# Four tiles for raw weights instead of two, each load issued four half units ahead

## The chip, the cores and the metric

The kernel runs on one core of one Trainium2 chip. The time is that of one execution on the device, in microseconds (us); the timed runs are three, and their median counts. The trace is of one further execution, the profiled one, which has a time of its own. Engines are named as the profile does: PE (TensorE, with its weight loads as PEld), DVE (VectorE), ACT (ScalarE), POOL (GpSimd), SP (SyncE, which here only issues DMA transfers).

## What is computed

Attention whose scores are mixed over the heads before and after the softmax, for 4 batches, 12 heads, 448 positions and a head size of 64, and behind it a two-layer network with a PReLU on the 1792 rows of 768 numbers that attention gives. `w_in` and `w_out` come as float64, all else as float32.

```python
scores = scale * np.matmul(q, k.transpose(0, 1, 3, 2))
scores = np.einsum('bhij,hg->bgij', scores, w_pre)
scores = scores - np.max(scores, axis=-1, keepdims=True)
attn = np.exp(scores)
attn = attn / (np.sum(attn, axis=-1, keepdims=True) + 1e-09)
attn = np.einsum('bhij,hg->bgij', attn, w_post)
attn_out = np.matmul(attn, v).astype(np.float32)
x = np.ascontiguousarray(attn_out.transpose(0, 2, 1, 3)).reshape(B * S, H * D)
h = x @ w_in
g = np.maximum(h, 0.0) + alpha * np.minimum(h, 0.0)
out = (g @ w_out).astype(np.float32)
```

## The kernel before

**Three kinds of work in one program.** The order of the instructions on every engine is fixed by the order of the code; each engine works in that order and waits where a tile isn't ready. The code is one loop over steps n (`step`). A step does one block of attention: the head mix on PE into PSUM (`mix`, L205), the negated maximum on DVE (`nm`, L207), the exponentials on ACT (`exp`, L214), for the block before it the scales on DVE (`norm`, L221 to L225), for the block two before it the second mix on PE (`post`, L238) and its copy on ACT (L244). Some steps have a QK product (L177) with its copy (L181, on ACT or DVE), and some a product with V (`pv`, L261), whose two halves of positions are copied by ACT (L267) and added by DVE (`xe`, L268). The scores go from one layout to the other by SBUF-to-SBUF transfers that SP issues (`relay`, `sr<-st`, four or more a step).

**The network** (`moe`) runs in tasks of one batch each, a few matmuls at a time between the parts of a step, from step `ready[0]` on; a table of paces (`PACE`) says how much per step. Its first layer is L394, its second L427; the weights come from a DRAM scratch `wsc` by `load_w` (`wr`, issued by POOL) and are split into two parts by ACT (L340) and POOL (`ws`, L341). DVE does the PReLU (`t`, L348 and L349, and L355) and sums the output (`acc`, L363).

**The conversion** (`convert`, `round_f64`) turns the float64 weights into float32 in `wsc`. It is cut into 64 half units: 16 blocks f, two weights x (0 is `w_in`, 1 is `w_out`), two halves c of 384 columns. A half unit has a raw tile `cr` (128 partitions of 384 float64, 384 KB in all), an exponent tile `ce` and a result tile `ct`. Its instructions: L60 (DVE, reads `cr`), L61 and L62 (POOL, on `ce`) with L64 (DVE, reads `cr`, writes `ct`), L65 (DVE, reads `cr`), L66 (DVE, the last to read `cr`), L67 (DVE, finishes `ct`). The generator yields five pieces a unit; a step before `ready[0]` takes 7 of them (`CONV_LEAD`), one after it 8 (`CONV_T0`). The pieces of neighbouring units are interleaved: L60 and L64 of unit i, then L66 and L67 of unit i - 1, then L65 of unit i.

With the L67 of unit i two transfers are tied. Its store to `wsc` (192 KB, L299) is put in a list and issued by SP at the end of the step (`flush`), behind the relays of that step. Its successor's load (`fetch_c`, L289) is issued by POOL at this place of the code, so behind L61 and L62 of unit i + 1; it must wait until the L66 of unit i has read the tile that it overwrites. The pool `cvp` has two tiles each for `cr`, `ce` and `ct`. So L60 of unit i + 2 waits for the load issued behind unit i, and L64 of unit i + 2 for the store of unit i.

POOL also issues, in the same program order, the loads of `q`, `k`, `v` and `wr`. SP issues the stores of `xe`, the loads of `xr` and the output.

Of the kernel before, what the change touches and what calls it, by code (L numbers as in the profile page):

```python
# [12 lines left out]
I64 = mybir.dt.int64  # L13
# [32 lines left out]
CU = DM // 2  # L46
# [3 lines left out]
def round_f64(nc, raw, e, t):  # L50

    w = raw.bitcast(I32).rearrange("p (n t) -> p n t", t=2)
    lo, hi = w[:, :, 0], w[:, :, 1]
    tf = t.bitcast(F32)
    v, g = nc.vector, nc.gpsimd

    yield lambda: v.tensor_scalar(out=e, in0=hi, scalar1=0x7FF00000, scalar2=None, op0=ALU.bitwise_and)  # L60
    g_clamp = lambda: g.tensor_scalar(out=e, in0=e, scalar1=float(1150 << 20), scalar2=float(916 << 20), op0=ALU.min, op1=ALU.max)  # L61
    g_scale = lambda: g.tensor_scalar(out=e, in0=e, scalar1=float(-(916 << 20)), scalar2=8.0, op0=ALU.add, op1=ALU.mult)  # L62
    yield lambda: (g_clamp(), g_scale(),
                   v.tensor_scalar(out=t, in0=hi, scalar1=0xFFFFF, scalar2=0x100000, op0=ALU.bitwise_and, op1=ALU.bitwise_or))  # L64
    yield lambda: v.scalar_tensor_tensor(out=tf, in0=lo.bitcast(U32), scalar=2.0 ** -32, in1=t, op0=ALU.mult, op1=ALU.add)  # L65
    yield lambda: v.scalar_tensor_tensor(out=e, in0=hi, scalar=-0x80000000, in1=e, op0=ALU.bitwise_and, op1=ALU.bitwise_or)  # L66
    yield lambda: v.tensor_tensor(tf, tf, e.bitcast(F32), ALU.mult)  # L67
# [3 lines left out]
def talking_heads_prelu(ctx: ExitStack, tc: tile.TileContext, q, k, v, w_pre, w_post, mask, w_in, w_out, alpha, out):  # L71
# [47 lines left out]
    cvp = pool("cvp", 2)  # L119
# [161 lines left out]
    def convert():  # L281
        todo = [(f, x, c) for f in range(NFC) for x in range(2) for c in range(0, DM, CU)]
        raw_c = {}

        def fetch_c(i):
            if i < len(todo):
                f, x, c = todo[i]
                raw_c[i] = cvp.tile([128, CU], I64, tag="cr", name=f"cr{f}_{x}_{c}")
                nc.gpsimd.dma_start(out=raw_c[i], in_=(w_in, w_out)[x][f, :, c:c + CU])  # L289

        def unit(i):
            f, x, c = todo[i]
            raw = raw_c.pop(i)
            e = cvp.tile([128, CU], I32, tag="ce", name=f"ce{f}_{x}_{c}")
            t = cvp.tile([128, CU], I32, tag="ct", name=f"ct{f}_{x}_{c}")
            for j, op in enumerate(round_f64(nc, raw, e, t)):
                op()
                if j == 4:
                    later.append(lambda: (stored.add((f, x, c)), nc.sync.dma_start(out=wsc[f, :, x * DM + c:x * DM + c + CU], in_=t.bitcast(F32))))  # L299
                    fetch_c(i + 2)  # L300
                yield

        fetch_c(0)
        fetch_c(1)
        yield
        n = len(todo)
        seq = []
        for i in range(n + 1):
            seq += [(i, 0), (i, 1)] if i < n else []
            seq += [(i - 1, 3), (i - 1, 4)] if i else []  # L310
            seq += [(i, 2)] if i < n else []
        units = {}
        for i, j in seq:
            if j == 0:
                units[i] = unit(i)
            next(units[i], None)
            yield
# [156 lines left out]
    with tc.manual_schedule():  # L474
# [41 lines left out]
        load_q(1)  # L516
        nc.gpsimd.dma_start(out=alpha_sb, in_=alpha)
        conv = convert()
        relayed = 0

# [136 lines left out]
```

## Time and profile before

| | us |
|---|---|
| timed runs: median (lowest to highest) | 1153.49 (1153.07 to 1157.48) |
| the profiled execution: time | 1158.48 |
| its span, from the first to the last instruction | 1156.7 |
| PE busy with matmuls (share of the span) | 911.7 (79%) |
| DVE busy | 605.3 (52%) |
| POOL busy | 486.9 (42%) |
| ACT busy | 422.0 (36%) |
| mean granted clock of PE, as a share of full speed | 0.876 |

The profile's page follows the chain of work that ended last back from the last instruction: each step of it is what released the step after it. By lines its largest shares are PE at L427 (17%) and L394 (16%), then the load `cr<-in_w_in_dram` (8%), the load `cr<-in_w_out_dram` (7%), PE at L238 (5%). In the rows further below, a time in square brackets behind an instruction is the idle time of its engine just before it, with what ended it; numbers of tiles are left out there (`cr` is any tile of that name). In a row of the timeline the first number is the start in us and the second the duration. An engine that is not named as waiting may still be idle because nothing was left in its order.

### The profile page before, as it was taken

To read this page: it belongs to the slowest core of one execution; us is meant where nothing else is said; L and a number is where in the kernel's file an instruction comes from. 1 tells how busy PE (TensorE), PEld (TensorE's weight loads), DVE (VectorE), ACT (ScalarE), POOL (GpSimd) and SP (SyncE) were. 2 spreads that over 40 slices of the span, in tenths; PEclk is the share of its full clock that TensorE was granted. 3 is DMA by queue.
4 is the path that set the end of the run, shared out by engine and by line. 5 is a ranking of instruction groups with operands and counts; after the bars stand their busy time and mean duration, and the time that the engine had idled before them with its cause. 6 is when DMAs were issued, how large, how long until landed. Compare 5 with 4: busy or idle time off the path is not lost.

```text
span 1156.7 us, 28915 instructions
## 1 busy us (share of the span) xinstructions
PE 911.7 (79%) x12204; PEld 711.3 (61%) x12204; DVE 605.3 (52%) x1090; ACT 422.0 (36%) x769; POOL 486.9 (42%) x563
## 2 busy tenths in 40 slices
PE   6446565364677766396989999999899999989997
PEld 3224343243454544364866878778678788869996
DVE  4456565553476455457554644463565445445443
ACT  2223333222133223143553555554264544313330
POOL 5332333324154434345342455443253334437662
PEclk8667676875688897698998999999899999989999
DMA  6654456456445445445464446444463333334322
GB/s 168 181 155 144 145 154 179 146 151 195 138 131 154 143 136 150 133 133 160 133 182 162 135 129 167 126 137 147 125 191 124 112 114 108 94 122 122 109 82 76
DMA packets 79730, 161.82 MB, mean 140 GB/s; under 512 B 26276, under 2 KB 64304, under 8 KB 79600
## 3 DMA queue, kind: packets, MB, share of 16 engines
q0 software_dynamic: 21312, 90.58, 29.3%
q1 hardware_dynamic: 57432, 68.18, 17.5%
q8 instruction: 96, 1.57, 0.6%
q10 hardware_dynamic: 856, 1.21, 0.4%
q14 instruction: 34, 0.28, 0.1%
HBM read 97.62 MB, written 23.59 MB: 105 GB/s over the span
## 4 chain that ended last, share of the span: by engine, by line
PE 49%; DMA 22%; DVE 10%; POOL 9%; issue 6%; ACT 1%; SPq 1%; POOLq 0%; ACTq 0%; DVEq 0%
PE p L427 17%; PE p L394 16%; DMA cr<-in_w_in_dram 8%; DMA cr<-in_w_out_dram 7%; PE p L238 5%; PE p L261 4%; POOL ws L341 4%; PE p L205 4%; PE p L177 3%; DMA wsc<-ct 3%; DMA sr<-st 2%; POOL ce L62 2%; DVE nm L207 2%; POOL ce L61 1%; DVE ce L60 1%
## 5 line engine op out<-in xcount | busy, mean ns | idle before, releaser
L341 POOL TENSOR_TENSOR ws<-wr,ws 128x768 fp32r<-128x768 f32 x128 | 235.8, 1843 | 283.6 <-ACT ws L340 281.8
L427 PE MATMUL p<-g,ws 128*128 128x448 f32 x1152 | 259.2, 379 | 21.6 <-POOL ws L341 14.1
L394 PE MATMUL p<-xs,ws 128*128 128x448 f32 x1152 | 262.2, 382 | 12.9 <-DVE xs L449 10.5
L427 PEld LDWEIGHTS p<-g,ws 128*128 128x128 f32 x1152 | 221.3, 195 | 62.0 <-POOL ws L341 18.4
L394 PEld LDWEIGHTS p<-xs,ws 128*128 128x128 f32 x1152 | 220.0, 195 | 57.9 <-issue 21.7
L238 PEld LDWEIGHTS p<-r,e 64*64 64x64 f32 x5040 | 120.2, 157 | 135.6 <-issue 70.7
L238 PE MATMUL p<-r,e 64*64 64x60 f32 x5040 | 125.5, 248 | 91.0 <-DVE r L225 36.3
L214 ACT ACTIVATE e<-p,nm 128x448 f32<-128x448 f32 x180 | 112.6, 633 | 228.1 <-DVE nm L207 172.7
L244 ACT COPY at<-p 128x960 f32<-128x960 f32 x88 | 86.4, 982 | 190.6 <-PE p L238 190.6
L340 ACT CAST ws<-wr 128x768 fp32r<-128x768 f32 x128 | 103.9, 844 | 122.9 <-issue 49.5
L205 PE MATMUL p<-sr,wk 64*64 64x448 f32 (+1 forms) x720 | 106.2, 627 | 53.3 <-ACT e L214 15.5
L207 DVE TENSOR_REDUCE nm<-p 128x2 f32<-128x896 f32 x90 | 97.6, 1084 | 87.0 <-PE p L205 87.0
L177 PE MATMUL p<-k,q 64*64 64x448 f32 x768 | 118.8, 674 | 30.6 <-DVE t L349 21.5
L60 DVE TENSOR_SCALAR ce<-cr 128x384 int32<-128x384 int32 x64 | 28.3, 442 | 208.9 <-DMA cr<-in_w_in_dram 129.9
L363 DVE TENSOR_TENSOR acc<-p,acc 128x896 f32<-128x896 f32 x84 | 91.3, 1087 | 87.9 <-PE p L427 87.7
L61 POOL TENSOR_SCALAR ce<-ce 128x384 int32<-128x384 int32 x64 | 34.8, 543 | 215.8 <-DVE ce L60 215.2
L261 PE MATMUL p<-at,v 64*64 64x120 f32 (+2 forms) x3360 | 98.5, 266 | 29.2 <-ACT e L214 22.9
L261 PEld LDWEIGHTS p<-at,v 64*64 64x64 f32 x3360 | 96.2, 148 | 41.0 <-ACT e L214 26.3
L348 DVE TENSOR_SCALAR t<-p,alpha_sb 128x448 f32<-128x448 f32 x64 | 43.4, 679 | 94.0 <-PE p L394 94.0
L332 POOL DMA_DIRECT2D wr<-wsc x128 | 71.9, 562 | 40.2 <-POOL ws L341 34.7
L205 PEld LDWEIGHTS p<-sr,wk 64*64 64x64 f32 (+1 forms) x720 | 29.8, 150 | 92.1 <-issue 32.5
L181 ACT COPY st<-p 128x896 f32<-128x896 f32 x84 | 74.9, 911 | 11.3 <-PE p L177 6.5
(48 smaller groups left out, 663.7 us busy)
## 6 DMA issues: line engine op xcount, KB each, us to landing
wr<-wsc POOLq DMA_DIRECT2D x128, 384.0 KB, 3.6
sr<-st SPq DMA_DIRECT2D x332, 105.0 KB
cr<-in_w_in_dram POOLq DMA_DIRECT2D x32, 384.0 KB, 4.1
cr<-in_w_out_dram POOLq DMA_DIRECT2D x32, 384.0 KB, 4.1
wsc<-ct SPq DMA_DIRECT2D x64, 192.0 KB
xr<-x SPq DMA_DIRECT2D x24, 224.0 KB
out_dram<-acc SPq DMA_DIRECT2D x12, 448.0 KB
q<-in_q_dram POOLq DMA_DIRECT2D x54, 90.0 KB, 3.7
```

Of the source, the lines that this page charges most:

```text
L177: nc.tensor.matmul(pt[64 * cc:64 * cc + 64, r, :S], q_t[ci][h, (3 * cc + p) * cn + SR0 * cc:(3 * cc + p) * cn + SR0 * cc + 64], k_t[b, p][ ...
L205: nc.tensor.matmul(to[hf:hf + 64, u, :S], wk[r, :], g[r, :], start=True, stop=True)
L207: nc.vector.tensor_reduce(out=nm, in_=to[:, :, :S], axis=AX.X, op=ALU.max, negate=True)
L214: nc.scalar.activation(out=e_t[n][:, u], in_=m_t[n][:, u, :S], func=AF.Exp, bias=nm_t[n][:, u:u + 1], scale=1.0, accum_out=se_t[n][:, u:u ...
L238: nc.tensor.matmul(dst[:, :, HI * u:HI * u + HI], e[h, u, 64 * jb:64 * jb + 64], r[h, u].rearrange("p (h i) -> p h i", h=H), start=True, s ...
L244: nc.scalar.copy(at[:, :, col:col + 2 * GI].rearrange("p q (g i) -> p g q i", g=2), pt[:, :, :NS * GP].rearrange("p g (q i) -> p g q i", i ...
L261: nc.tensor.matmul(to[64 * t:64 * t + 64, r, cl * cn:(cl + 1) * cn], v_t[b, hx][pr, s, (2 * cl + t) * D:(2 * cl + t + 1) * D], a_t[pr, s, ...
L340: nc.scalar.copy(t[:, 0], w)
L341: nc.gpsimd.tensor_tensor(t[:, 1], w, t[:, 0], ALU.subtract)
L363: nc.vector.tensor_tensor(dst, pt[:, :, :N], dst, ALU.add)
L394: nc.tensor.matmul(pt[:, f % 2, :S], w[:, tw, c * 128:(c + 1) * 128], xs[:, tx, c, :], start=(j == 0), stop=(j == 3 * NCC - 1))
L427: nc.tensor.matmul(pt[:, d, :S], w[:, tw, (c + d) * 128:(c + d + 1) * 128], g[:, tg], start=(j == 0), stop=(j == 3 * FG - 1))
```

## The change

The tiles named `cr` get four buffers of their own instead of the pool's two. Four loads are issued ahead of the first unit instead of two, and the load tied to the end of unit i is that of unit i + 4 instead of unit i + 2. All else, `ce` and `ct` with their two buffers among it, is as it was.

```diff
@@ -285,7 +285,7 @@
         def fetch_c(i):
             if i < len(todo):
                 f, x, c = todo[i]
-                raw_c[i] = cvp.tile([128, CU], I64, tag="cr", name=f"cr{f}_{x}_{c}")
+                raw_c[i] = cvp.tile([128, CU], I64, tag="cr", bufs=4, name=f"cr{f}_{x}_{c}")
                 nc.gpsimd.dma_start(out=raw_c[i], in_=(w_in, w_out)[x][f, :, c:c + CU])
 
         def unit(i):
@@ -297,11 +297,11 @@
                 op()
                 if j == 4:
                     later.append(lambda: (stored.add((f, x, c)), nc.sync.dma_start(out=wsc[f, :, x * DM + c:x * DM + c + CU], in_=t.bitcast(F32))))
-                    fetch_c(i + 2)
+                    fetch_c(i + 4)
                 yield
 
-        fetch_c(0)
-        fetch_c(1)
+        for i in range(4):
+            fetch_c(i)
         yield
         n = len(todo)
         seq = []
```

On DVE, SP, ACT and PE the rows are the same ones in the same order. On POOL the loads move. This is POOL at the start of the conversion, before the change (a name has block, weight and column of its half unit, and last a number of the tile: `cr0_1_384` is block 0, `w_out`, columns from 384):

```order
L289 DMA cr0_0_0_228<-in_w_in_dram 128x384
L289 DMA cr0_0_384_230<-in_w_in_dram 128x384
L160 DMA q2_128<-in_q_dram 64x2x180 x2
L160 DMA q0_126<-in_q_dram 64x2x180 x2
L61 ISA
L61 TENSOR_SCALAR ce0_0_0_242<-ce0_0_0_242 128x384
L62 TENSOR_SCALAR ce0_0_0_242<-ce0_0_0_242 128x384
L61 TENSOR_SCALAR ce0_0_384_249<-ce0_0_384_249 128x384
L62 TENSOR_SCALAR ce0_0_384_249<-ce0_0_384_249 128x384
L289 DMA cr0_1_0_257<-in_w_out_dram 128x384
```

And the same place after it:

```order
L289 DMA cr0_0_0_228<-in_w_in_dram 128x384
L289 DMA cr0_0_384_230<-in_w_in_dram 128x384
L289 DMA cr0_1_0_232<-in_w_out_dram 128x384
L289 DMA cr0_1_384_234<-in_w_out_dram 128x384
L160 DMA q2_128<-in_q_dram 64x2x180 x2
L160 DMA q0_126<-in_q_dram 64x2x180 x2
L61 ISA
L61 TENSOR_SCALAR ce0_0_0_246<-ce0_0_0_246 128x384
L62 TENSOR_SCALAR ce0_0_0_246<-ce0_0_0_246 128x384
L61 TENSOR_SCALAR ce0_0_384_253<-ce0_0_384_253 128x384
L62 TENSOR_SCALAR ce0_0_384_253<-ce0_0_384_253 128x384
L289 DMA cr1_0_0_261<-in_w_in_dram 128x384
```

Two loads now stand ahead of the two pairs of `q` loads, and the load behind the first units is that of block 1.

The second place is POOL where the first weights for the network are loaded and split, around 260 to 277 us of the trace. Before the change:

```order
L332 DMA wr0_0_2321<-wsc_58 128x768
L332 DMA wr0_1_2323<-wsc_58 128x768
L332 DMA wr1_0_2325<-wsc_58 128x768
L332 DMA wr1_1_2327<-wsc_58 128x768
L341 TENSOR_TENSOR ws0_0_2329<-wr0_0_2321,ws0_0_2329 128x768
L332 DMA wr2_0_2332<-wsc_58 128x768
L341 TENSOR_TENSOR ws1_0_2334<-wr1_0_2325,ws1_0_2334 128x768
L332 DMA wr3_0_2337<-wsc_58 128x768
L289 DMA cr9_0_0_2401<-in_w_in_dram 128x384
L61 TENSOR_SCALAR ce9_0_0_2404<-ce9_0_0_2404 128x384
L62 TENSOR_SCALAR ce9_0_0_2404<-ce9_0_0_2404 128x384
```

After it:

```order
L332 DMA wr0_0_2325<-wsc_58 128x768
L332 DMA wr0_1_2327<-wsc_58 128x768
L332 DMA wr1_0_2329<-wsc_58 128x768
L332 DMA wr1_1_2331<-wsc_58 128x768
L341 TENSOR_TENSOR ws0_0_2333<-wr0_0_2325,ws0_0_2333 128x768
L332 DMA wr2_0_2336<-wsc_58 128x768
L341 TENSOR_TENSOR ws1_0_2338<-wr1_0_2329,ws1_0_2338 128x768
L332 DMA wr3_0_2341<-wsc_58 128x768
L289 DMA cr9_1_0_2405<-in_w_out_dram 128x384
L61 TENSOR_SCALAR ce9_0_0_2408<-ce9_0_0_2408 128x384
L62 TENSOR_SCALAR ce9_0_0_2408<-ce9_0_0_2408 128x384
```

The place of the load is the same; before the change it is the load of the unit whose L61 follows it (`ce9_0_0`), after it that of two units later, and the load for `ce9_0_0` stands two loads further up.

## Rows read from the trace of the kernel before

**Rows 1.** Busy time of each engine in three stretches, in us.

```profile
core 0: us, PE busy (x) PEld busy (x) DVE busy (x) ACT busy (x) POOL busy (x), PEclk, DMA share, GB/s
15.00:300.00 285.00, 154.15 (x2956) 104.61 (x2952) 150.11 (x321) 84.84 (x171) 98.47 (x162) 0.70 0.56 164
300.00:545.00 245.00, 164.48 (x1819) 120.88 (x1820) 143.74 (x257) 73.57 (x134) 105.89 (x134) 0.81 0.48 141
545.00:1157.00 612.00, 583.60 (x7391) 480.62 (x7389) 304.65 (x489) 260.51 (x461) 271.11 (x242) 0.98 0.44 129
```

**Rows 2.** Waits of DVE, 15 to 300 us: total us, times, longest.

```profile
DVE ce L60 <- DMA cr<-in_w_in_dram: 71.7, 20, 12.3
DVE ce L60 <- DMA cr<-in_w_out_dram: 48.8, 19, 6.8
DVE ct L64 <- DMA wsc<-ct: 6.8, 6, 1.8
```

**Rows 3.** Waits of DVE, 300 to 545 us.

```profile
DVE ce L60 <- DMA cr<-in_w_in_dram: 58.2, 11, 10.4
DVE ce L60 <- DMA cr<-in_w_out_dram: 30.2, 10, 7.2
```

**Rows 4.** Waits of PE, 300 to 545 us.

```profile
PE p L177 <- DVE t L349: 21.5, 4, 7.6
PE p L238 <- DVE xe L268: 18.0, 2, 12.2
PE p L205 <- ACT e L214: 15.5, 5, 6.1
```

**Rows 5.** Pieces of the chain: start us, us, what; first relays, two stores.

```profile
13.97 8.07 DMA sr<-st
...
75.25 4.03 DMA wsc<-ct
...
144.35 2.81 DMA wsc<-ct
```

**Rows 6.** Timeline of DVE and SP, first stretch: start, duration, engine, line.

```profile
78.89 0.36 DVE L60 TENSOR_SCALAR ce<-cr 128x384 int32<-128x384 int32 x1 [1.61 <-DMA cr<-in_w_in_dram]
79.30 0.36 DVE L64 TENSOR_SCALAR ct<-cr 128x384 int32<-128x384 int32 x1
79.58 0.86 DVE L66 SCALAR_TENSOR_TENSOR ce<-cr,ce 128x384 int32<-128x384 int32 x1
...
81.24 0.33 SPq L299 DMA_DIRECT2D wsc<-ct  x1
...
85.04 0.36 DVE L60 TENSOR_SCALAR ce<-cr 128x384 int32<-128x384 int32 x1 [3.36 <-DMA cr<-in_w_out_dram]
...
88.23 0.35 DVE L64 TENSOR_SCALAR ct<-cr 128x384 int32<-128x384 int32 x1
...
229.09 0.36 DVE L60 TENSOR_SCALAR ce<-cr 128x384 int32<-128x384 int32 x1 [3.03 <-DMA cr<-in_w_out_dram]
```

**Rows 7.** Timeline of ACT and DVE around the longest wait.

```profile
276.11 0.24 ACT L267 COPY xe<-p 128x90 f32<-128x90 f32 x1 [2.33 <-PE p L261]
276.36 0.36 DVE L60 TENSOR_SCALAR ce<-cr 128x384 int32<-128x384 int32 x1 [12.29 <-DMA cr<-in_w_in_dram]
...
280.05 0.40 DVE L268 TENSOR_TENSOR xe<-p,xe 128x90 f32<-128x90 f32 x2
```

**Rows 8.** Timeline of DVE: three waits in the second stretch.

```profile
431.96 0.36 DVE L60 TENSOR_SCALAR ce<-cr 128x384 int32<-128x384 int32 x1 [7.33 <-DMA cr<-in_w_in_dram]
...
443.19 0.36 DVE L60 TENSOR_SCALAR ce<-cr 128x384 int32<-128x384 int32 x1 [7.48 <-DMA cr<-in_w_in_dram]
...
485.98 0.36 DVE L60 TENSOR_SCALAR ce<-cr 128x384 int32<-128x384 int32 x1 [8.30 <-DMA cr<-in_w_in_dram]
```

**Rows 9.** Timeline of POOL and DVE at 320 us.

```profile
320.12 1.92 POOL L341 TENSOR_TENSOR ws<-wr,ws 128x768 fp32r<-128x768 f32 x1
320.27 2.17 DVE L66 SCALAR_TENSOR_TENSOR ce<-cr,ce 128x384 int32<-128x384 int32 x1
```

## The prediction

> **What bounds the kernel now.** I read the stretches first [rows 1], because a share of the whole span would mix three kinds of work. Up to 300 us no engine is busy for more than 154 of 285 us; from 300 to 545 us PE is busy for 164 of 245. The change can act only in these two, since the conversion of the weights ends with the second. After 545 us PE's granted clock is 0.98 and it is busy nearly throughout: what is won before is kept, and nothing is added there.
>
> In the first stretch DVE is busy for 150.1 us and waits 71.7 + 48.8 = 120.5 us at L60, the first read of a `cr` tile, for its load [rows 1, 2]; that is nearly all the time there is. In the second it waits 58.2 + 30.2 = 88.4 us at the same line [rows 3]. Everything else that DVE has to do (the maxima L207, the softmax scales, the additions L268, the PReLU) is queued behind these waits in program order, and PE then waits for DVE [rows 4]. So 209 us of waiting seems to be there for the taking.
>
> **What stands right behind it.** The row after L60 decides how much. A half unit i ends with L66 (last read of `cr`) and L67 (writes `ct`); L66 releases the next load on POOL, L67 the store of `ct` on SP. Unit i+2 needs both: L60 the load, L64 the same `ct` tile, whose store must have landed. There are two `ct` tiles before and after the change. In the chain the store issued at 75.25 us takes 4.03 us, to 79.28, and L64 starts at 79.30; L60 had waited for its load until 78.89 [rows 5, 6]. Load and store return together: without any wait at L60, that L64 would start at 79.28 as well. This unit wins nothing. The lines between are the same for all units, so this is the normal case, and the number of tiles of `cr` doesn't touch it.
>
> **The change, part by part.**
>
> *Two tiles more, and loads two half units earlier.* No instruction is added or taken away. On POOL the load stands where it stood, behind the same L61 and L62 and released by the same L66; only its contents are for a unit two further on. So the wait of POOL is as it was, and no load, `q`, `v` or `wr` issue gets another transfer ahead of it, but for the start. The 64 waits at L60 should nearly vanish from the third unit on: the load is issued more than two units (some 12 us at the pace of [rows 6]) ahead of its use, and as seen it lands when the store beside it does, after about 4.
>
> *Start.* Two loads go out with the first two that went out behind the L66 of units 0 and 1. They share the DMA engines with the first relays, one of which takes 8.07 us in the chain [rows 5], and two `q` loads are issued behind them. The bound is nothing on one side, and on the other half of that relay's time, as if the four loads took twice what two take: loss 0 to 4. I take **2 us**, because the relays also wait for copies.
>
> *First stretch, where the step's boundary falls between L60 and L64.* The conversion emits 7 instructions a step and 5 a unit, so every seventh unit has the whole softmax part of a step between its L60 and its L64. There the wait at L60 delays work that needs no store. At 85.04 L60 had waited 3.36 us, and its L64 came at 88.23; the store it needs was issued at 81.24 and would be back at 81.24 + 4.0 = 85.2 [rows 6]. Gain 3.0 us. There are five such places before 260 us; at the last of them, 229.09, L60 waited 3.03 [rows 6]. More than that none can give, and where SP issues the store late, behind four relays, it is less. I take three quarters, 2.3 us each: **11.5 us** (7.5 to 15).
>
> *The gap of 12.29 us at 276.36* [rows 7]. The load stood on POOL behind four `wr` issues and two subtractions. With the load long there, L60 starts at 264, but L268 behind it needs ACT's copy of PV sums, which ended at 276.35; it started at 280.05. Gain **3.7 us** (0 to 12.3), since that copy depends on PE, not on the conversion.
>
> *Second stretch.* Here units lie further apart, and the store has often landed before L60 gets its load. What is then won is what PE waits less. Two places carry most of it. First, L60 waits 7.33 us at 431.96 and 7.48 at 443.19 [rows 8], the loads having stood on POOL behind weight subtractions; the longest waits of PE for `e` (6.1) and for `t` (7.6) follow them [rows 4]. Sum 13.7, less than the 14.8 of L60's. Second, L60 at 485.98 waits 8.30 us, and PE's longest wait for `xe` (12.2) [rows 4, 8] ends with the L268 behind it. I take 8.3 and the 2 that the unit before gives up: 10.3. Together **24 us**. PE's other waits for `t`, `xe` and `e` come to 21.5 + 18.0 + 15.5 - 7.6 - 12.2 - 6.1 = 29.1 us [rows 4]. They are behind L60 waits of 1 to 10 us, of which some end with the store; I take half, **14 us** (0 to 29).
>
> Not counted: the granted clock of 0.81 in that stretch against 0.98 later [rows 1] is a mean of stretches at 1.2 and at 2.4 GHz; if half of the difference came back, 164 x 0.17 / 0.98 / 2 = 14 us more. It is in the range only.
>
> **Sum.** 11.5 + 3.7 + 24 + 14 - 2 = 51 us. The profiled execution took 1158.48 us with a span of 1156.7; that is 5 us (0.4%) above the median of the timed runs, 1153.49. The sum gives 1107 for a profiled execution and **1102 us** for the median. Bounds: without the 14, with half of the 24, with 7.5 for 11.5 and 4 for 2, 51 - 14 - 12 - 4 - 2 = 19 is left, 1134; with all 29 and the clock it is 51 + 15 + 14 = 80, 1073.
>
> **The rivals.**
>
> *The store gets faster too.* A store is back after 2.81 us at 144.35, against 4.03 at 75.25 [rows 5]; the load of that unit had gone out earlier. If stores no longer ran beside loads, each of the 39 units with a wait in the first stretch [rows 2], less the 6 counted above, would be 1.2 us shorter: 33 x 1.2 = 40 more, 1062. Against it: load and store are issued one instruction apart, as before.
>
> *All of it goes.* If `ct` never waited, the first stretch would lose about 115 us and the second PE's 55 us of waits for DVE [rows 4]: 1153 - 170 = 983. Against it stands the pair at 78.89 and 79.30, and 6.8 us of waits for the store that show already now [rows 2].
>
> *The second stretch gives it back.* POOL's subtractions and ACT's casts are in program order with what comes earlier; if PE then waits for `ws` instead, only the first stretch and a fourth of the second stay: 15 + 10 - 2 = 23, 1130.
>
> *Nothing happens.* Every unit is bound by its store as closely as the one at 79.30, or the loads are still issued late: 1151.
>
> *Slower: DVE and POOL get in each other's way.* At 320.27 an L66 takes 2.17 us beside a POOL subtraction that started at 320.12 [rows 9]; at 79.58, without one, 0.86 [rows 6]. A stretched instruction costs the 1.3 us between them, and the second stretch has about 25 units x 5 = 125 such instructions. If DVE, no longer waiting for loads, runs in step with POOL's subtractions where now it waits while they run, the loss passes the 51 won from 40 stretched instructions more; at 50 it is 65, and the time 1153 + 14 = 1167. Against it: POOL is busy for 106 of 245 us only [rows 1], so fewer than half should meet. The Trainium skill (SBUF — State Buffer, Who interferes with whom) has a rule for this: a DVE instruction with two inputs in SBUF contends with a GpSimd instruction that reads SBUF, and by the summary there the later of the two blocks until the first is done. By that rule a meeting costs DVE up to a whole subtraction, and the 2.17 us agrees with it; how many meet, it doesn't say.
>
> **How the numbers follow.** Forecast 1102, chance 0.56. Store faster, 1062: 0.12. All of it, 983: 0.04. Given back, 1130: 0.17. Nothing, 1151: 0.05. Slower, 1167: 0.06. The range 1055 to 1134 takes in the forecast's bounds and the first and third rivals, and leaves out 0.04 + 0.05 + 0.06 and a little of the tails. About 0.5% (6 us) is what a measurement of this kernel can tell from no change. Faster by more: 0.56 + 0.12 + 0.04 + 0.17 = 0.89; same 0.05; slower 0.06.
>
> **What would show it.** Right: waits of L60 for `cr` fall from 209 us to under 30, and waits of L64 for `wsc<-ct`, now 8, rise to over 80, most of them before 300 us; the second stretch loses more than the first; PE's wait of 12.2 us for `xe` is gone; the time after the conversion's end is as before. Wrong: L64 waits little (then the store was not next); L60 still waits; PE waits for `ws` L341 by tens of us more; or the instructions at L60 to L67 grow in mean duration.

## The result, and the profile after

The changed kernel takes 1091.66 us (median of 4 runs, 1086.72 to 1092.34); the kernel before takes 1153.28 us beside it. The ratio is 0.945, 95% interval 0.941 to 0.949: 62 us, or 5.5%, faster. The profiled execution of after took 1092.34 us with a span of 1090.5, against 1156.7 before, so the two traces lie 66.2 us apart; 5 of these are the amount by which the profiled execution of before stood above its median.

First the waits of DVE over the whole span of after: total us, times, longest.

```profile
DVE ct L64 <- DMA wsc<-ct: 132.7, 52, 8.6
...
DVE ce L60 <- DMA cr<-in_w_in_dram: 3.9, 1, 3.9
```

The 209 us of waits for `cr` [rows 2, 3] are gone but for 3.9. In their place 52 of the 64 half units wait at L64 for the store of `ct`, where 8 us stood before. In the stretch from 15 to 265 us of after, which ends one half unit short of the first stretch of before, it is

```profile
DVE ct L64 <- DMA wsc<-ct: 92.4, 35, 8.6
```

against the 120.5 us of [rows 2]; from 265 to 490 us it is 40.2 against 88.4 [rows 3]. Over half of the wait has only changed its name, 133 us of 209, and 92 of these 133 lie before 265 us. The timeline of after (start, duration, engine, line) shows how for the half unit that stood at 78.89 in [rows 6]:

```profile
73.65 0.33 SPq L299 DMA_DIRECT2D wsc<-ct  x1
...
75.60 0.35 DVE L60 TENSOR_SCALAR ce<-cr 128x384 int32<-128x384 int32 x1
...
77.63 0.36 DVE L64 TENSOR_SCALAR ct<-cr 128x384 int32<-128x384 int32 x1 [1.68 <-DMA wsc<-ct]
...
78.75 0.60 POOL L289 DMA_DIRECT2D cr<-in_w_in_dram  x1 [1.61 <-DVE ce L66]
...
79.08 0.33 SPq L299 DMA_DIRECT2D wsc<-ct  x1
```

L60 doesn't wait any more. L64 comes 2.0 us behind it, and for 1.68 of these DVE waits for the store issued at 73.65; before, the two stood 0.4 us apart (78.89 and 79.30 [rows 6]), with the wait in front of L60. Load and store still go out 0.33 us apart (78.75 and 79.08). The chain of after says what the store costs; start us, us:

```profile
73.65 3.96 DMA wsc<-ct
79.08 3.92 DMA wsc<-ct
84.46 3.92 DMA wsc<-ct
...
163.09 10.87 DMA wsc<-ct
```

Between 15 and 265 us the chain goes through 28 such stores, with a median of 3.99 us: no shorter than the 4.03 of [rows 5].

Where the time went is read from the start of the same L64 in both traces:

| half unit | before | after | difference |
|---|---|---|---|
| 2 | 27.87 | 30.57 | +2.7 |
| 3 | 36.71 | 36.34 | -0.4 |
| 35 | 259.49 | 245.29 | -14.2 |
| 36 | 276.64 | 254.75 | -21.9 |
| 40 | 320.00 | 295.84 | -24.2 |
| 51 | 420.61 | 379.89 | -40.7 |
| 53 | 448.04 | 397.64 | -50.4 |
| 55 | 464.72 | 413.59 | -51.1 |
| 57 | 488.73 | 426.59 | -62.1 |
| 63 | 538.43 | 472.30 | -66.1 |

The maxima of all later steps stay 66 us ahead. For the part behind half unit 40, and for all that follows the conversion, these are the stretches of before with the same work (columns as in [rows 1]):

```profile
320.00:540.30 220.30, 148.60 (x1776) 109.63 (x1775) 129.31 (x228) 67.74 (x122) 103.08 (x130) 0.83 0.49 143
...
540.30:1156.00 615.70, 587.44 (x7409) 483.84 (x7407) 308.79 (x498) 263.46 (x467) 271.11 (x242) 0.98 0.44 129
```

and of after:

```profile
295.80:474.10 178.30, 140.45 (x1775) 105.41 (x1775) 133.77 (x227) 67.83 (x122) 100.98 (x128) 0.90 0.60 173
...
474.10:1090.00 615.90, 586.71 (x7409) 483.80 (x7407) 308.89 (x498) 263.35 (x467) 270.71 (x242) 0.98 0.44 129
```

The last stretch is as it was. The one before it is 42.0 us shorter: 8.2 us because PE was busy for less time with the same matmuls (granted clock 0.90 instead of 0.83), 33.8 us because it stood idle less. The waits of PE in after, 265 to 490 us, agree:

```profile
PE p L177 <- DVE t L349: 8.2, 3, 5.2
PE p L238 <- DVE xe L268: 7.7, 2, 5.7
...
PE p L205 <- ACT e L214: 5.4, 4, 2.8
```

Together 21.3 us against 55.0 in [rows 4], 33.7 less.

### The profile page after: what moved, and what is told of

Read it like the earlier page. It is cut to its first block, busy times and chain, and to the rows that moved or that the text cites. A ratio compares the mean times of both kernels' runs of the same rounds, so it can differ in the third digit from the quotient of the medians.

```text
span 1090.5 us, 28930 instructions
## 1 busy us (share of the span) xinstructions
PE 894.5 (82%) x12204; PEld 701.7 (64%) x12204; DVE 604.7 (55%) x1090; ACT 421.5 (39%) x769; POOL 480.0 (44%) x563
## 4 chain that ended last, share of the span: by engine, by line
PE 53%; DMA 22%; DVE 14%; issue 4%; POOL 2%; SPq 2%; ACT 1%; ACTq 0%; POOLq 0%; DVEq 0%
PE p L427 18%; PE p L394 17%; DMA wsc<-ct 17%; PE p L261 5%; PE p L238 5%; PE p L205 4%; PE p L177 4%; DVE ce L66 3%; DVE ct L67 3%; DMA sr<-st 2%; DVE ct L64 2%; POOL ws L341 2%; DVE nm L207 2%; SPq L198 1%; DMA xr<-x 1%
## 5 line engine op out<-in xcount | busy, mean ns | idle before, releaser
L394 PE MATMUL p<-xs,ws 128*128 128x448 f32 x1152 | 258.9, 379 | 10.2 <-DVE xs L449 8.0
L238 PEld LDWEIGHTS p<-r,e 64*64 64x64 f32 x5040 | 113.7, 149 | 113.0 <-issue 68.9
L238 PE MATMUL p<-r,e 64*64 64x60 f32 x5040 | 119.5, 239 | 71.8 <-DVE r L225 34.0
L340 ACT CAST ws<-wr 128x768 fp32r<-128x768 f32 x128 | 103.9, 844 | 117.8 <-issue 51.9
L177 PE MATMUL p<-k,q 64*64 64x448 f32 x768 | 115.7, 655 | 23.0 <-DVE xe L268 8.4
L205 PE MATMUL p<-sr,wk 64*64 64x448 f32 (+1 forms) x720 | 102.5, 608 | 38.0 <-ACT at L249 12.4
L64 DVE TENSOR_SCALAR ct<-cr 128x384 int32<-128x384 int32 x64 | 29.7, 464 | 132.7 <-DMA wsc<-ct 132.7
L61 POOL TENSOR_SCALAR ce<-ce 128x384 int32<-128x384 int32 x64 | 33.4, 521 | 78.0 <-DVE ce L60 76.4
```

Source lines behind the costliest of these rows:

```text
L177: nc.tensor.matmul(pt[64 * cc:64 * cc + 64, r, :S], q_t[ci][h, (3 * cc + p) * cn + SR0 * cc:(3 * cc + p) * cn + SR0 * cc + 64], k_t[b, p][ ...
L205: nc.tensor.matmul(to[hf:hf + 64, u, :S], wk[r, :], g[r, :], start=True, stop=True)
L238: nc.tensor.matmul(dst[:, :, HI * u:HI * u + HI], e[h, u, 64 * jb:64 * jb + 64], r[h, u].rearrange("p (h i) -> p h i", h=H), start=True, s ...
L340: nc.scalar.copy(t[:, 0], w)
L394: nc.tensor.matmul(pt[:, f % 2, :S], w[:, tw, c * 128:(c + 1) * 128], xs[:, tx, c, :], start=(j == 0), stop=(j == 3 * NCC - 1))
```

## The experiments

**Theory**: two half units ahead there are two transfers, load and store, that return together. The change takes the load out of the wait, and what is left is the store, which runs beside a load and so takes 4 us. **Rivals**: the store is not what holds the first stretch, and more tiles of `ct` bring nothing more; or the four tiles matter as such; or POOL, which stands with its load behind L66, is what holds it.

### Three tiles for `cr`, four for `ct`

```diff
-  tag="cr", bufs=4 ... fetch_c(i + 4)
+  tag="cr", bufs=3 ... fetch_c(i + 3)
-  t = cvp.tile([128, CU], I32, tag="ct", ...
+  t = cvp.tile([128, CU], I32, tag="ct", bufs=4, ...
```

> Three raw tiles with loads three half units ahead, and four result tiles ct instead of two (four of each don't fit the memory left). My theory: in the changed kernel DVE waits for the store of ct where it waited for the load (132.7 us at L64 in its profile), so with two more result tiles these waits fall under 10 us, and the first 300 us shorten again. The DMA engines were busy for 0.62 of 250 us there, so they alone need 155 us, and DVE 143: the stretch ends near 180 us instead of 250. Expected 1025 us (1005 to 1060). Rival: the store is only what the wait is booked on, and another thing is due just behind it (the relays that SP issues, the exponentials on ACT): then less than 20 us are won, 1075 to 1095.

Measured: 1012.85 us, ratio to before 0.878 (0.873 to 0.882); 79 us below the changed kernel. Waits at L60 are 23.4 us, at L64 1.2. The store was the next wait, and its place is not taken by another of like size.

### Four tiles for `ct` alone

The kernel before, with `bufs=4` for `ct` and nothing else.

> The kernel before with four result tiles ct, its raw tiles and loads unchanged. My theory: the load is due as late as the store at every unit, so this alone takes away the 8.2 us of waits at L64 and nothing else: 1150 us (1143 to 1154), and L60 waits 205 to 212 us for its loads. Rival: the store was the binding one from the start, and the raw tiles only follow it: 1100 or less.

Measured: 1150.09 us, ratio 0.996 (0.994 to 0.998). The waits of DVE in it:

```profile
DVE ce L60 <- DMA cr<-in_w_in_dram: 130.7, 31, 11.7
DVE ce L60 <- DMA cr<-in_w_out_dram: 76.3, 28, 7.5
```

207 us at L60 as before, none at L64. The same tiles that bring 79 us behind the change bring 5 (4.7 of 1154.8) without it: the tiles of `ct` count only where those of `cr` are there too.

### Three tiles for `cr` instead of four

`bufs=3`, three loads ahead, `fetch_c(i + 3)`.

> Three raw tiles, loads three half units ahead; result tiles two, as in both kernels. My theory: a load takes 4 us and a half unit at least 5.4, so one more half unit of lead hides it wherever POOL issues it in time; only where POOL is held up by weight subtractions (the waits of 7 to 12 us) the second one counts. Expected 1096 us (1090 to 1106), with 4 to 30 us of waits left at L60. Rival: it is the distance that counts, and half of it gives half: about 1122.

Measured: 1088.95 us, ratio 0.943 (0.940 to 0.947): the interval of the changed kernel overlaps it, and the time is just below the range that I had given. Waits are 7.8 us at L60 and 126.9 at L64. The fourth tile brings nothing that these runs can tell; one unit of lead is enough.

### Four tiles for `cr`, loads still two units ahead

`bufs=4`, with `fetch_c(i + 2)` as before the change. The load overwrites a tile that was last read two units earlier, so that it no longer waits for L66.

> Four raw tiles, but loads still issued two half units ahead, so that the load no longer waits for the last reader of its tile. My theory: the load keeps its place on POOL, behind L61 and L62 of the unit before, and goes out at most 0.6 us earlier; POOL's waits at the load vanish, L60 still waits over 180 us. Expected 1143 us (1130 to 1153). Rival: the wait for a free tile was what made the load late: 1100 or less.

Measured: 1119.37 us, ratio 0.970 (0.966 to 0.974). This missed: it brings 35 us of the 62 where I had expected 12. The waits of DVE:

```profile
DVE ce L60 <- DMA cr<-in_w_in_dram: 93.3, 29, 12.0
DVE ce L60 <- DMA cr<-in_w_out_dram: 54.3, 20, 7.4
...
DVE ct L64 <- DMA wsc<-ct: 28.2, 23, 2.9
```

and two stores of its chain:

```profile
124.69 2.43 DMA wsc<-ct
131.73 2.48 DMA wsc<-ct
```

Here the load goes out 1.84 us ahead of the first of these stores and 3.61 us ahead of the second, and the store is back sooner. The median of its 13 stores in the chain between 15 and 265 us is 3.00 us, not 3.99. That made the theory sharper: the store is long *because* the load goes out with it.

### The changed kernel without its later loads

```diff
+  if i < 4:
+      first_c[i] = cvp.tile([128, CU], I64, tag=f"cr{i}", bufs=1, ...)
+      nc.gpsimd.dma_start(out=first_c[i], ...)
+  raw_c[i] = first_c[i % 4]
```

> The changed kernel without the loads of raw weights from the fifth on: all later half units convert the first four tiles again, so the weights that the network uses are wrong, and everything else is done as before, every store among it. My theory: a store comes back after 3.5 us because its unit's load runs beside it, and after 2.3 to 2.9 alone; DVE waits for the store at some 35 places in the first stretch, so that about 35 x 0.9 = 30 us go there and some 10 in the second: 1050 us (1035 to 1070), waits of DVE at L64 under 100 us instead of 133. Rival: the relays that SP issues next, not the load, are what the store shares the DMA engines with: then it keeps its 3.5 us, and the time 1082 to 1092.

Measured: 1029.43 us, ratio 0.890 (0.888 to 0.893). The gain went past what I had expected. Of the 20 stores in its chain between 15 and 265 us, 12 take under 2.2 us, the shortest 1.84; waits at L64 are 67.9 us. But this kernel takes away three things: the bytes, the issues on POOL, and the waits of these issues for L66.

### The bytes of the loads alone

The kernel above, but with every load issued in its place, and of 8 columns only:

```diff
+  else:
+      nc.gpsimd.dma_start(out=first_c[i % 4][:, 0:8], in_=(w_in, w_out)[x][f, :, c:c + 8])
```

> The changed kernel with every instruction of POOL kept in its place, every load with its wait for L66 among them, but from the fifth half unit on a load brings only 8 of the 384 columns (8 KB instead of 384). The rest of the tile keeps the numbers of the unit four before, so the converted weights are wrong; the work on every engine is that of the changed kernel. Only the bytes that move beside the stores are gone. Theory (the bytes of the load are what stretches the store): stores of the chain near 1.85 to 2.6 us, waits at L64 of 60 to 90 us against 132.7, and a time near that of the kernel without these loads, 1029, plus at most 15 for the waits of POOL that are back: 1036 (1029 to 1048). Rival (the kernels with freed or missing loads gained because POOL no longer stood behind L66): the time stays at 1075 to 1092 and POOL still waits some 120 us at the load, with stores at 3.5 to 4.0 us. Between 1048 and 1075 both have a part, and the split is read from it.

Measured: 1033.71 us, ratio 0.896 (0.893 to 0.898), where the theory had 1036 and the rival 1075 to 1092. The chain has

```profile
73.43 2.17 DMA wsc<-ct
78.53 1.85 DMA wsc<-ct
```

at about the time of the 3.96 and 3.92 above; the median of its 20 stores is 2.23 us. Ten of them go out 0.32 to 0.38 us behind a load, as the first of these two does, and their median is 2.2 us; in the changed kernel 22 stores go out as close behind a load of 384 KB, with a median of 4.0. The waits of DVE and of POOL:

```profile
DVE ct L64 <- DMA wsc<-ct: 66.2, 31, 4.9
```

```profile
POOL cr L292 <- DVE ce L66: 66.8, 27, 4.8
```

POOL still waits 66.8 us at its load (L292 here, with the added lines), and it costs little. So of the 62 us between the changed kernel (1091.7) and the one without loads (1029.4), 58 belong to the bytes of the loads, and with these gone some 4 to POOL (57 and 7 by the ratios to before). The waits at L64 fall by 66.5 us, so the store is the main way by which the bytes cost time. It isn't shown to be the only one: without them the median load of `v` (576 KB) is back 6.5 us after its issue instead of 9.0 and that of `q` (90 KB) 3.2 instead of 4.3, and what this is worth was not separated. The Trainium skill (DMA: Bandwidth & Descriptors, Issuing engines are not separate DMA queues) says that transfers started by different engines run on the same 16 DMA engines and interleave; a store from SP that takes 4.0 us beside a load from POOL agrees with it. In which order the packets were served is not read from these traces.

### Four tiles, load freed of L66, one unit less ahead

`bufs=4`, three loads ahead, `fetch_c(i + 3)`.

> Four raw tiles, loads three half units ahead: there is always a free tile, so a load no longer waits for L66 but goes out right behind L62, about 1.2 us before L66 ends, and so ahead of the store instead of with it. My theory: as in the kernel with four tiles and loads two ahead, a store then comes back after 2.9 us instead of 3.55; at some 33 units in the first stretch that is 20 us: 1069 us (1060 to 1080). Rival: once DVE no longer waits for loads it doesn't matter when they go out: as with three tiles, 1086 to 1092.

Measured: 1066.25 us, ratio 0.921 (0.917 to 0.925), the time as expected: 25 us faster than the change at the same memory. Waits at L64 are 99.9 us instead of 132.7. The stores fell less than expected: the median of the 26 in the chain is 3.49 us, against 3.99 in the changed kernel and the 2.9 of the theory.

### Four tiles, load moved behind the store

```diff
-                    fetch_c(i + 4)
+                if j == 1 and i >= 2: fetch_c(i + 2)
```

> The changed kernel with its load moved behind the store: cr keeps four tiles, but the load tied to unit i is issued on POOL right behind L61 and L62 of unit i and is for unit i + 2, into the tile that unit i - 2 has long left. It no longer waits for L66, and it goes out about 1.9 us after a store instead of 0.3 us before it (in the changed kernel the store went out at 79.08 and L62 of the next unit ended at 80.98). Theory (a load that goes out together with a store is what stretches the store from 1.85 to 4.0 us): the stores of the chain take 1.9 to 2.8 us, waits at L64 fall from 132.7 to 50 to 85 us, waits at L60 stay under 30, and the time is 1050 (1035 to 1070). First rival (the kernels with freed loads gained because POOL no longer stood behind L66, and the meeting of load and store matters little): stores of the chain at 3.3 to 4.0 us, as in the changed kernel, and a time from 1066, as with the load freed and put early, to 1085. Second rival (the load is now late: it has under two units left and L60 waits again): L60 over 60 us, time 1080 to 1110.

Measured: 1073.96 us, ratio 0.929 (0.925 to 0.933). This missed, for two reasons. On POOL the place is nearly that of the kernel above: there too the load follows L62 of the same unit, and only what POOL has to do at the end of a step comes between. And behind one store is ahead of the next, as its timeline shows:

```profile
69.10 3.65 SPq L299 DMA_DIRECT2D wsc<-ct  x2
...
71.06 0.58 POOL L289 DMA_DIRECT2D cr<-in_w_out_dram  x1
...
75.97 0.60 POOL L289 DMA_DIRECT2D cr<-in_w_out_dram  x1
...
77.21 0.33 SPq L299 DMA_DIRECT2D wsc<-ct  x1
```

and its chain:

```profile
69.10 1.85 DMA wsc<-ct
72.42 3.32 DMA wsc<-ct
77.21 2.53 DMA wsc<-ct
```

The store of 69.10 is back before the next load goes out and takes 1.85 us. Those of 72.42 and 77.21 go out 1.36 and 1.24 us behind a load and take 3.32 and 2.53. Of the 25 stores of this chain, the six that go out less than 0.4 us behind a load take 3.9 to 8.8 us, the five at 1.2 to 1.4 us take 2.5 to 4.5, and the eleven at 2.8 us or more take 1.8 to 4.6, with a median of 2.6. At some 5 us a unit, a load of 4 us can't keep clear of every store. By its total this run tells the theories apart no better than the one before it, and why it is 8 us slower than that one is open; store by store it leans to the first theory, with much scatter.

### Three tiles for both

`bufs=3` for `cr` and for `ct`, `fetch_c(i + 3)`.

> Three raw tiles and loads three ahead, with three result tiles. My theory: with one more result tile a store has a whole half unit more, over 4 us, which is more than its 3.5 to 4.1 us, so that nearly all is won that four give (1013 us): 1020 us (1010 to 1035), waits at L64 under 20 us. Rival: at the faster pace a unit takes 4 us and stores queue behind relays on SP, so the fourth tile still carries a third of it: 1040.

Measured: 1013.03 us, ratio 0.876 (0.874 to 0.878), like the kernel with four tiles of `ct`. It takes 1.5 KB a partition less memory than the change (a tile of `cr` is 3 KB a partition, one of `ct` 1.5: three and three are 13.5 KB, four and two 15 KB) and is 79 us faster. Its waits at L60 are 19.7 us, at L64 9.2. This beats both kernels.

## Why the prediction was right, and where not

It forecast 1102 us and 51 us of gain; it became 1092 and 62 between the medians (66.2 between the traces).

**What bounds, and what stands behind it**: right. The wait moved from L60 to L64, as the pair of 78.89 and 79.30 had shown [rows 6]; 133 us of 209 came back. That the store is really what is left, the kernels with more tiles of `ct` show.

**Start**, +2: it measured +2.7 at half unit 2, and the first gain gives it back.

**The five places with a step's boundary**, -11.5: half units 3, 10, 17, 24 and 31 come 3.1, 3.5, 2.0, -0.6 and 2.0 us closer to the one before, together 10.1. The loss at 24 is the store issued at 163.09, which took 10.87 us in the chain. The other units of the first stretch, costed at nothing, gave 6.8 between them, 0.2 each in the mean. (Half unit 4 lost 3.5 and half unit 5 gave 3.8, so for the first units only the sum is sure.)

**The gap at 276.36**, -3.7: mis-sized, 7.7. The step that failed is "that copy depends on PE, not on the conversion". Rows of before show on what PE's mix depended there (POOL, ACT, PE):

```profile
260.87 2.18 POOL L332 DMA_DIRECT2D wr<-wsc  x4
...
264.35 0.83 ACT L340 CAST ws<-wr 128x768 fp32r<-128x768 f32 x1 [13.65 <-DMA wr<-wsc]
...
269.24 1.77 PE L205 MATMUL p<-sr,wk 64*64 64x448 f32 x8 [12.88 <-ACT at L249]
```

The same in after, with L64 of half unit 35:

```profile
241.09 2.18 POOL L332 DMA_DIRECT2D wr<-wsc  x4
245.29 0.36 DVE L64 TENSOR_SCALAR ct<-cr 128x384 int32<-128x384 int32 x1 [5.45 <-DMA wsc<-ct]
247.34 0.83 ACT L340 CAST ws<-wr 128x768 fp32r<-128x768 f32 x1 [10.19 <-DMA wr<-wsc]
...
251.83 1.77 PE L205 MATMUL p<-sr,wk 64*64 64x448 f32 x8 [12.42 <-ACT at L249]
```

ACT holds PE up (L249 stands behind the cast L340), the cast waits for `wr`, and POOL issues `wr` behind L61, which waits for L60. L60 is free now, so POOL is 19.8 us ahead, while DVE, which stops at L64, is 14.2 ahead. The cast came 6.3 us behind the issue of `wr` instead of 3.5, so PE's mix gained 17.4. I had followed the conversion's waits on DVE only; that what stands behind L61 on POOL is freed even where L64 waits was missed.

**The second stretch**, -24 and -14: from half unit 40 on 42.0 us, of which 33.8 are waits of PE (38 forecast) and 8.2 the clock. By place: half units 51 to 53 gave 9.7 (13.7 forecast) and 55 to 57 gave 11.0 (10.3), both with their part of the clock. PE's waits there, before:

```profile
446.11 3.27 PE L177 MATMUL p<-k,q 64*64 64x448 f32 x16 [7.63 <-DVE t L349]
...
488.43 1.97 PE L238 MATMUL p<-r,e 64*64 64x60 f32 x56 [12.16 <-DVE xe L268]
```

and after:

```profile
393.59 3.27 PE L177 MATMUL p<-k,q 64*64 64x448 f32 x16 [0.77 <-DVE t L349]
...
426.29 1.15 PE L238 MATMUL p<-r,e 64*64 64x60 f32 x56 [2.00 <-DVE xe L268]
```

The wait of 12.2 fell to 2.0, and the same 56 matmuls took 1.15 us instead of 1.97, at a granted clock of 1.00 instead of 0.50, the higher of its two levels (2.4 GHz) instead of the lower (1.2 GHz). Half units 36 to 40, which the forecast had no term for, gave 2.3. The sum of what was seen is -2.7 + 10.1 + 6.8 + 7.7 + 2.3 + 42.0 = 66.2. So what the forecast lacked of that is 6.8 in small gains, 4.0 in the gap, 2.3 behind it and 8.2 of clock, which stood in its range alone. Against that, PE's waits gave 4.2 less than forecast, the boundaries 1.4 less, and the start cost 0.7 more: 15 in all, from 51 to 66.

**A statement that was wrong**: "So the wait of POOL is as it was". By the waits of POOL over the whole span it is, before,

```profile
POOL ce L61 <- DVE ce L60: 215.2, 56, 13.9
...
POOL cr L289 <- DVE ce L66: 39.1, 20, 4.4
```

and after:

```profile
POOL cr L289 <- DVE ce L66: 120.8, 45, 8.1
POOL ce L61 <- DVE ce L60: 76.4, 45, 13.2
```

The wait at the load trebled, since L66 now stands behind the wait at L64 and L61 no longer behind one at L60. Together the two fell from 254 to 197 us, and the kernel with the tiny loads shows that what is left of it at the load costs little. The number was harmless, the reasoning was not: a wait that moves on one engine moves on those that follow it.

**The rivals.** *The store gets faster too*: not in this kernel (3.99 us), for the reason given. Its mechanism is real all the same: without the bytes of the loads it is 58 us rather than 40. *All of it goes*, 983: with both buffers deep it is 1013; 30 us of what I had added up as waits are taken by others behind them, and I have not followed them further. *Given back*: no, PE's waits for `ws` didn't grow (1.7 us from 265 to 490, 2.8 before from 300 to 545). *Slower, DVE against POOL*: no. Up to the end of the conversion L66 is busy for 43.0 us in 63 instructions (46.4 before), L65 for 37.5 (41.0), L67 for 41.7 (40.3), L60 for 26.1 (28.3); only L64 grew clearly, to 29.7 (24.7). The five together went from 180.7 to 178.0 us. Meetings with a subtraction on POOL did become more: three L66 took 2.2 us, where one did before. And the price of one was read too low: the 0.86 us at 79.58 [rows 6] stood beside L61 and L62 on POOL, while an L66 with nothing beside it takes 0.55 (at 88.50 in before), so that a meeting costs 1.6 us rather than 1.3.

## What to carry to other kernels

Where an engine waits for one of two transfers that return together, a deeper buffer for one moves the wait to the other; look one instruction behind the wait, and give the same memory to both (three and three tiles: 1013 us, against 1092 for four and two). Ask too when the early transfer goes out: if it is released a moment before the late one, as here by L66 with L67 right behind it, they run side by side, and the late one comes back later (a store 0.3 us behind a load: 4.0 us, or 2.2 where the load brings next to no bytes). And follow what is freed on every engine that stands behind the wait, not only on the one that waits.

## What was not expected of the hardware

A store of 192 KB that takes 1.84 us at its fastest with no load of weights in flight, and 2.1 in the median of that chain, takes 4.0 us in the median when a load of 384 KB has gone out 0.3 to 0.4 us before it on another engine, and 2.5 to 4.5 us when the load is 1.2 to 1.4 us ahead. That the two are issued on different engines doesn't keep them apart: with the load's bytes gone and all else in place, the kernel was 58 us faster.
